# First loads cut smaller, fewer cleared rows and an earlier third block in a talking-heads attention with a dense block behind it

## Chip, cores and metric

One core of one Trainium2 chip runs the whole program in one launch. The metric is the device time in microseconds (us), the median of several runs. Beside it stands one profiled execution, from which all rows below come.

## What is computed

```python
scores = scale * q @ k^T                                  # 4 batches, 12 heads, 448 x 448, depth 64
scores = einsum('bhij,hg->bgij', scores, w_pre)           # heads mixed before the softmax
attn   = softmax(scores, axis=-1)
attn   = einsum('bhij,hg->bgij', attn, w_post)            # heads mixed after it
x      = (attn @ v), heads side by side                   # 1792 x 768
h      = x @ w_in                                         # 768 x 2048
out    = where(h > 0, h, exp(min(h, 0)) - 1) @ w_out      # 2048 x 768
```

The two weights of the dense part come as float64 and are turned into float32 on the chip ("decoding").

## The kernel before

**Blocks and steps.** Each batch is cut into four blocks of rows of the score matrix (`BLK`: 10, 12, 12 and 11 groups of ten rows). A group's ten rows times twelve heads make 120 rows of an on-chip tile, and mixing heads is then one matmul with a 60-row weight per half. The blocks n = 0 to 15 are worked off in 92 steps of two groups each (5, 6, 6, 6 steps for a batch). All of it is written out in one loop, `for j in range(-LOOK, N + 3)`, with `LOOK = 2`, and each engine runs its instructions strictly in that order.

**What a step does.** Step j issues, in this order: the mixed scores of step j+2 (`scores`, L251, with the row maximum on VectorE, L256, and the exponential on ScalarE, L258); the sends of the raw scores made one step before (`send`, L240); the product with the values for a block that is finished (`av`, L303); raw scores of a later block (`qk`, L213 or L220, with copies out of PSUM, L230); the mixing behind the softmax of step j (`post`, L282, whose weight `wz` GpSimd scales, L271) and its copy (`keep_post`, L289); then planned pieces of work.

**Raw scores and how they travel.** `qk(n, hp)` makes block n's raw scores for the head pair hp. For blocks 0 and 1 it uses the float32 queries and keys as they are; from block 2 on queries and keys are first split in a high part (VectorE: `qh`, `kh`, L197, L185) and a low part (GpSimd: `ql`, `kl`, L198, L186). Each head's result is copied to a tile `st` (or, at the start, to a `room` borrowed from tiles that are not yet in use) and sent by a DMA into every twelfth row of one of two tiles `raws`; block n uses `raws[n % 2]`. The first scores of a block need the sends of all twelve heads. Block 0 is sent in two parts, four groups first, then six. Its odd heads go through GpSimd's queue, everything else through SyncE's (SP). Rows of `raws` that no head fills are cleared at the start: before the change whole tiles were, by VectorE and GpSimd, ahead of the sends.

**Where the order comes from.** `RAW_AT` gives the steps of a batch in which a block's raw scores are made (two head pairs at a time), `OUT_AT` those of the product with the values; `plan(j, f)` puts loads and splits into a step. Queries are loaded five steps ahead of their first use and split two steps ahead, the keys' splits stand at the same distance. Values of batch 0 are loaded in steps 2 to 7, one head pair each, through GpSimd's queue.

**Dense part.** `Weights` decodes 48 pieces of the weights in four small steps each (`dec.step()`), in every second step of the attention from 20 on, and then inside `Moe.elu` and the loops behind it; a piece is stored to HBM and loaded again as a weight tile `lo`, which ScalarE and GpSimd split (L509, L510) before TensorE uses it (L593).

Of the kernel before, what the change touches and what calls it, by code (L numbers as in the profile page):

```python
# [126 lines left out]
def attention(ctx, tc, qd, kd, vd, wpre, wpost, xd, dec, moe):  # L127
# [61 lines left out]
    def load_q(n, eng):  # L189
        q2[n] = ld.tile([128, NP, 120], F32, tag="q2", name="q2")  # L190
        eng.dma_start(out=q2[n], in_=qd[blocks[n]])
# [42 lines left out]
    def send(n, out, t0=0, t1=None):  # L234
        t1 = t1 or slots[n]
        raw = raws[n % 2][:, t0:t1, :]
        for h, st in out:
            eng = nc.gpsimd if n == 0 and h % 2 else nc.sync
            lo = FRONT + h
            eng.dma_start(out=raw[lo:lo + (R - 1) * H + 1:H], in_=st[t0 * R:t1 * R])  # L240
# [3 lines left out]
    def scores(n, ts):  # L244
        z = small.tile([128, 2], F32, tag="z", name="z")
        got = []
        ps = [bank("s", mixes) for _ in ts]
        for w in range(2):
            for a in range(len(ts)):
                half = slice(a * 64, (a + 1) * 64)  # L250
                nc.tensor.matmul(  # L251
                    ps[a][w * 64:(w + 1) * 64, :S], wa[half], raws[n % 2][half, ts[0] + w, :],
                    start=True, stop=True)
        for i in range(len(ts)):
            nm = small.tile([128, 1], F32, tag="nm", name="nm", bufs=6)
            nc.vector.tensor_reduce(nm, ps[i][:, :S], op=ALU.max, axis=AX.X, negate=True)  # L256
            p = pp.tile([128, S], F32, tag="p", name="p")
            nc.scalar.activation(  # L258
                p, ps[i][:, :S], AF.Exp, bias=nm, scale=1.0, accum_out=z[:, i:i + 1])
            got.append(p)  # L260
        return got, z
# [61 lines left out]

    warm = pp.tile([128, S], F32, tag="p", name="warm")
    nc.vector.memset(warm, 0.0)
    nc.vector.memset(raws[0][:, :FIRST], 0.0)
    nc.gpsimd.memset(raws[0][:, FIRST:], 0.0)
    nc.gpsimd.memset(raws[1][:, NP:], 0.0)
    k0 = atp.tile([128, NJ * 12 * RH], F32, tag="at", name="k0")[:, :NP * S].rearrange("p (h s) -> p h s", h=NP)
    load_q(0, nc.sync)  # L330
    for hp, eng in ((4, nc.scalar), (2, nc.sync), (0, nc.scalar)):
        eng.dma_start(out=k0[:, hp:hp + 2], in_=kd[0, hp:hp + 2].rearrange("h p s -> p h s"))
        for w in range(2):
            k2[0, hp + w] = k0[:, hp + w]
    load_q(1, nc.sync)
    wa = cst.tile([128, 64], F32, name="wa")
    wb = cst.tile([128, RH // 2], F32, name="wb")
    nc.sync.dma_start(out=wa, in_=wpre)
    nc.sync.dma_start(out=wb, in_=wpost)
    for n in (S, S, 128):  # L340
        nc.tensor.matmul(bank("s", six)[:120, :n], warm[:, :120], warm[:, :n], start=True, stop=True)
    nc.vector.memset(raws[1][:, :NP], 0.0)
    for ps in mixed:
        nc.scalar.copy(ps[64:, 0, NJ - 1], warm[64:, :RH // 2])
        nc.scalar.copy(ps[:64, 1, NJ - 1], warm[:64, :RH // 2])
    nc.vector.tensor_scalar_mul(wa, wa, 1.0 / float(np.sqrt(D)))
    rooms = [vp.tile([128, NJ * CJ], F32, tag="v", name="room")[:120, :S] for _ in range(8)]
    rooms += [xp.tile([128, NP * 120], F32, tag="x", name="room")[:120, :S] for _ in range(2)]
    rooms += [ld.tile([128, S], F32, tag="k2", name="room", bufs=4)[:120] for _ in range(2)]
# [1 line left out]
    for hp in (4, 5, 2, 3, 0, 1):  # L351
        got = keep_qk(0, [(hp, qk(0, hp))], rooms)
        send(0, got, 0, FIRST)
        out += got
    send(0, out, FIRST)
    for hp in range(4):
        send(1, keep_qk(1, [(hp, qk(1, hp))]))
# [15 lines left out]
    OUT_AT = [(6, 8, 10), (12, 14, 16), (18, 20, 22), (23, 25, 27)]  # L373
    for n in range(1, NBL):
        b, i = blocks[n]
        at = [b * ROUND + j for j in (RAW_AT[i] if n > 2 else (None, (0, 0, 0), (2, 4, 6))[n])]
        for u in range(2 if n == 1 else 0, 3):
            qks.setdefault(at[u], []).append((n, u))
        if n > 1:
            plan(max(at[0] - 5, 1 - LOOK), lambda n=n: load_q(n, nc.gpsimd))  # L380
        if n > 1:
            plan(at[0] - 2, lambda n=n: split_q(n, nc.vector.tensor_copy, nc.gpsimd))
        if i == (0 if b else 2):
            for hp in range(NP):
                t = at[hp // 2] - bool(b)
                if b:
                    plan(t - 5, lambda b=b, hp=hp: load_k(b, hp, nc.gpsimd))
                plan(t - 2 + hp % 2, lambda b=b, hp=hp: split_k(
                    b, hp, nc.vector.tensor_copy, nc.gpsimd))
# [6 lines left out]
                for w in range(2):  # L396
                    plan(j + w, lambda b=b + 1, hp=2 * u + w: load_v(b, hp))
    for hp in range(NP):
        plan(hp + 2, lambda hp=hp: load_v(0, hp))

    DENSE = {N - 3: (0, 0), N - 1: (0, 1), N: (1, 0), N + 1: (1, 1), N + 2: (2, 0)}
    sc, nz, ready = {}, {}, []
    for j in range(-LOOK, N + 3):
        if j == N - 10:
            op_ctx.close()
            moe.begin()
            spare = [(moe.ps[0], f"ps{i}") for i in (2, 3)]
        if j >= N - 10:
            mixes = [(ps_s, "s0"), (ps_s, "s1")] if (N - j) % 2 else [(moe.ps[0], "ps0"), (moe.ps[0], "ps1")]
        if j == N - 2:  # L410
            s_ctx.close()
            raw_ctx.close()
            moe.begin_elu()
        if j == N:
            spare = [(ps_t, f"t{i}") for i in range(2)]
        if j in DENSE and j >= N:
            moe.first(*DENSE[j])
        if j + LOOK - 1 in sc:
            nz[j + LOOK - 1] = norm(*sc.pop(j + LOOK - 1))
        if 0 <= j + LOOK < N:  # L420
            sc[j + LOOK] = scores(*steps[j + LOOK])
        for n, out in ready:
            send(n, out)
        for n, u in avs.get(j, ()):
            for w in range(2):
                av(n, 2 * u + w)
            keep_av(n, u)
        ready = [(n, keep_qk(n, [(hp, qk(n, hp)) for hp in (2 * u, 2 * u + 1)], rooms)) for n, u in qks.get(j, ())]
        if j in nz:
            post(nz.pop(j))  # L430
            keep_post(*steps[j])
        if LATE <= j < 3 * ROUND and j % 2 == 0:
            dec.step()
        for f in work.get(j, ()):
            f()
        if N - 10 <= j < N:
            moe.loads(j - (N - 10))
        if N - 7 <= j < N:
            moe.ahead(j - (N - 7))
        if j in DENSE and j < N:  # L440
            moe.first(*DENSE[j])
        if j >= N - 1:
            moe.elu_first(j - N + 1)


class Moe:
# [150 lines left out]
    def elu(self, h, f, u):  # L597
        nc = self.nc

        g = self.ep.tile([128, S], F32, tag="g", name="g", bufs=4)  # L600
        nc.scalar.activation(g, h, AF.Relu, scale=-1.0)  # L601
        e = self.eps.tile([128, 512], F32, tag="e", name="e")[:, :S]
        nc.scalar.activation(e, g, AF.Exp, scale=-1.0)
        nc.scalar.activation(g, g, AF.Tanh, scale=-0.5)
        self.dec.step(3 + (u and f < 4))
        nc.vector.scalar_tensor_tensor(g, e, 1.0, g, op0=ALU.add, op1=ALU.mult)  # L606
        nc.vector.tensor_max(g, g, h)
        self.keep()
        self.last = g, f, u
# [510 lines left out]
```

## Time and profile before

| | us |
|---|---|
| median of 3 runs | 815.98 (814.39 to 818.77) |
| profiled execution, its own time | 811.92 |
| its span, first to last instruction | 810.1 |
| TensorE matmul busy | 780.5 (96%) |
| VectorE, ScalarE, GpSimd busy | 581.2, 509.3, 401.3 |

The 1.8 us between the span and the execution's own time lie around the program. Busy time of TensorE counts matmuls in flight, at whichever of its two clock levels (1.2 and 2.4 GHz) they ran; what ends its idle time is in the waits.

### The profile page before, as it was taken

Reading aid. Unit: us, or ns where it says so; the run is one execution under the profiler, and the core shown is the slowest. Engines: PE = TensorE matmul, PEld = TensorE weight load, DVE = VectorE, ACT = ScalarE, POOL = GpSimd, SP = SyncE. Lnnn points to the kernel's source line nnn. Section 1 sums busy time; section 2 is a strip of 40 time slices with the busy share of each in tenths; the row PEclk is TensorE's granted clock in tenths of the full one; section 3 lists DMA queues with packets and bytes.
Section 4 is the critical chain, followed back from the end, with each engine's and each line's share of the span. In section 5 each row is a group of like instructions: output and inputs, shape, how many; then the busy total and the mean of one; then the engine's idle time right before and its main releaser. Section 6 shows DMA issues by size and latency. Waiting matters only on the chain.

```text
span 810.1 us, 25135 instructions
## 1 busy us (share of the span) xinstructions
PE 780.5 (96%) x10014; PEld 630.4 (78%) x10014; DVE 581.2 (72%) x1082; ACT 509.3 (63%) x1092; POOL 401.3 (50%) x527
## 2 busy tenths in 40 slices
PE   7888998999899989999999999999999999999998
PEld 3355676666676766688799999999999999999997
DVE  5787666877687756667998886766556777688962
ACT  3676877777788768874787772233157576665440
POOL 6575544663557342254777772265238787600000
PEclk9899999999999999999999999999999999999999
DMA  6576577866776665837998879988535768553331
GB/s 196 187 221 216 166 230 241 246 197 202 251 238 184 217 207 157 237 112 244 331 313 273 282 243 340 309 304 300 192 120 190 228 215 268 187 166 116 116 123 58
DMA packets 92749, 174.60 MB, mean 216 GB/s; under 512 B 21792, under 2 KB 59460, under 8 KB 92632
## 3 DMA queue, kind: packets, MB, share of 16 engines
q1 hardware_dynamic: 75288, 113.46, 43.6%
q0 software_dynamic: 16800, 58.61, 22.7%
q8 instruction: 79, 1.29, 0.7%
q10 hardware_dynamic: 544, 0.92, 0.3%
q14 instruction: 38, 0.31, 0.1%
HBM read 94.04 MB, written 39.35 MB: 165 GB/s over the span
## 4 chain that ended last, share of the span: by engine, by line
PE 50%; DVE 1%; DMA 1%; issue 1%; ACT 1%; POOL 0%; DVEq 0%; ACTq 0%
PE y L688 15%; PE y L1042 13%; PE h L980 13%; PE h L593 10%; DMA s<-c 1%; DVE c L94 0%; POOL lo L510 0%; DVE g L606 0%; DVE room L80 0%; POOL gl L616 0%; ACT gh L615 0%; ACT g L601 0%; ACT hi L509 0%; DVE room L85 0%; ACT sq L89 0%
## 5 line engine op out<-in xcount | busy, mean ns | idle before, releaser
L256 DVE TENSOR_REDUCE nm<-s 128x1 f32<-128x448 f32 x180 | 103.8, 618 | 60.8 <-PE s L251 60.5
L258 ACT ACTIVATE p<-s,nm 128x448 f32<-128x448 f32 x180 | 112.6, 631 | 50.3 <-DVE nm L256 49.5
L271 POOL TENSOR_SCALAR wz<-wb,rz 128x60 f32<-128x60 f32 x180 | 79.5, 453 | 106.3 <-DVE rz L267 81.4
L289 ACT COPY at<-mixed 128x480 f32<-128x480 f32 (+1 forms) x184 | 93.3, 566 | 34.3 <-PE mixed L282 32.6
L282 PEld LDWEIGHTS mixed<-wz,p 64*64 64x64 f32 x5040 | 85.1, 135 | 35.0 <-issue 24.6
L282 PE MATMUL mixed<-wz,p 64*64 64x60 f32 x5040 | 98.6, 222 | 7.5 <-issue 6.1
L251 PE MATMUL s<-raw,wa 64*64 64x448 f32 x720 | 93.8, 559 | 12.3 <-DMA raw<-st 5.6
L303 PEld LDWEIGHTS xo<-at,v 128*64 128x64 f32 x1536 | 75.9, 135 | 33.9 <-ACT st L230 24.0
L1042 PE MATMUL y<-part,hi 128*128 128x448 f32 x336 | 96.4, 367 | 0.0
L303 PE MATMUL xo<-at,v 128*64 128x120 f32 (+2 forms) x1536 | 86.8, 263 | 1.6 <-DMA v<-in 1.6
L509 ACT CAST hi<-lo 128x1024 fp32r<-128x1024 f32 (+1 forms) x49 | 47.9, 978 | 41.1 <-PE y L1042 34.2
L593 PE MATMUL h<-xh,lo 128*128 128x448 f32 x192 | 70.7, 368 | 1.9 <-POOL lo L510 1.9
L980 PE MATMUL h<-op,hi 128*128 128x448 f32 x264 | 72.3, 367 | 0.0
L593 PE MATMUL h<-xh,hi 128*128 128x448 f32 x192 | 71.0, 370 | 0.0
L688 PE MATMUL y<-gh,lo 128*128 128x448 f32 x192 | 70.6, 367 | 0.0
L688 PE MATMUL y<-gl,hi 128*128 128x448 f32 x192 | 70.5, 367 | 0.0
L688 PE MATMUL y<-gh,hi 128*128 128x448 f32 x192 | 70.5, 367 | 0.0
L593 PE MATMUL h<-xl,hi 128*128 128x448 f32 x192 | 70.5, 367 | 0.0
L1042 PEld LDWEIGHTS y<-part,hi 128*128 128x128 f32 x336 | 63.0, 188 | 6.3
L510 DVE TENSOR_TENSOR lo<-lo,hi 128x1024 fp32r<-128x1024 f32 x30 | 37.6, 1253 | 42.1 <-ACT hi L509 39.9
L980 PE MATMUL h<-op,lo 128*128 128x448 f32 x240 | 67.3, 367 | 0.0
L1042 PE MATMUL y<-part,lo 128*128 128x448 f32 x168 | 61.8, 368 | 0.0
(121 smaller groups left out, 1647.2 us busy)
## 6 DMA issues: line engine op xcount, KB each, us to landing
raw<-st SPq DMA_DIRECT2D x140, 210.0 KB
w<-in POOLq DMA_DIRECT2D x48, 512.0 KB, 5.9
lo<-s SPq DMA_DIRECT2D x58, 256.0 KB
s<-c POOLq DMA_DIRECT2D x48, 256.0 KB, 5.1
raw<-st SPq DMA_DIRECT2D x36, 175.0 KB
v<-in POOLq DMA_DIRECT2D x24, 256.0 KB, 7.0
lo<-half SPq DMA_DIRECT2D x16, 384.0 KB
lo<-sum SPq DMA_DIRECT2D x12, 512.0 KB
```

Source lines behind the costliest of these rows:

```text
L251: nc.tensor.matmul(ps[a][w * 64:(w + 1) * 64, :S], wa[half], raws[n % 2][half, ts[0] + w, :], start=True, stop=True)
L256: nc.vector.tensor_reduce(nm, ps[i][:, :S], op=ALU.max, axis=AX.X, negate=True)
L258: nc.scalar.activation(p, ps[i][:, :S], AF.Exp, bias=nm, scale=1.0, accum_out=z[:, i:i + 1])
L271: nc.gpsimd.tensor_scalar_mul(wz, wb, rz[:, i:i + 1])
L282: nc.tensor.matmul(mixed[w][half, i, c, :], p[part, j * 64:(j + 1) * 64], wz[part], start=True, stop=True)
L289: nc.scalar.copy(ats[n][:, :, ts[0]:ts[0] + len(ts), w, :], mixed[w][:, :len(ts)].rearrange("p t c n -> p c t n"))
L303: nc.tensor.matmul(ps[hh * 64:(hh + 1) * 64, w * m:(w + 1) * m].rearrange("p (t r) -> p t r", r=HR), vs[blocks[n][0], hp][:, c, hh * 64:(h ...
L509: self.nc.scalar.copy(hi_, f32(lo_))
L593: self.nc.tensor.matmul(h, w[:, ks], x[:, k, :], start=n == 0, stop=n == 3 * NC - 1)
L688: nc.tensor.matmul(y[u], w[:, ks], g[f][:, u, :], start=f == 0 and n == 0, stop=f == NF - 1 and n == 2)
L980: nc.tensor.matmul(y, p[:, ks], x[:, z], start=q < 2 and k == 0 and n == 0, stop=k == KH - 1 and n == 2, skip_group_check=True)
L1042: nc.tensor.matmul(y, w[:, ks], g[:, x], start=begun is None and k == 0 and n == 0, stop=k == FH - 1 and n == 2, skip_group_check=True)
```

## The change

Eight things change.

- **First loads.** The queries of block 0 come in two loads (head pairs 4 and 5, then 0 to 3) instead of one; the keys of pairs 4 and 5 in one load each, one on ScalarE's queue and one on SP's, instead of one load of both; pairs 2 and 3 now go through ScalarE's queue and 0 and 1 through SP's.
- **Cleared rows.** Only the first `FRONT` = 4 rows of each `raws` tile are cleared, over all 5376 columns, both by GpSimd: `raws[0]` ahead of everything, `raws[1]` at the first step. The last four rows are not cleared, and the second half's matmul reads 60 rows instead of 64.
- **Warm-up.** Two matmuls on zeros instead of three (448 and 128 columns).
- **Scaling of `wa`** (the weight that mixes heads) stands on VectorE behind the copies of block 0's raw scores instead of ahead of them.
- **Third block** (n = 2): raw scores in steps 1, 3 and 5 instead of 2, 4 and 6; with them the splits of its queries and of the keys, one step earlier, and the load of its queries, one step earlier. The fourth block's queries are loaded in step 3 instead of 2.
- **Values of batch 0**: loaded in steps 1, 2, 4, 5, 5, 6 instead of 2 to 7.
- **Decoding in the attention** goes on for eight more steps (four more calls).
- **Decoding in `elu`**: the extra call stands at f = 0, 4, 8, 12 instead of f = 0, 1, 2, 3.

```diff
-                half = slice(a * 64, (a + 1) * 64)
+                half = slice(a * 64, a * 64 + (64, RH // 2)[a])
...
-    nc.vector.memset(raws[0][:, :FIRST], 0.0)
-    nc.gpsimd.memset(raws[0][:, FIRST:], 0.0)
-    nc.gpsimd.memset(raws[1][:, NP:], 0.0)
+    nc.gpsimd.memset(raws[0][:FRONT], 0.0)
...
-    load_q(0, nc.sync)
-    for hp, eng in ((4, nc.scalar), (2, nc.sync), (0, nc.scalar)):
-        eng.dma_start(out=k0[:, hp:hp + 2], in_=kd[0, hp:hp + 2].rearrange("h p s -> p h s"))
-        for w in range(2):
-            k2[0, hp + w] = k0[:, hp + w]
+    q2[0] = ld.tile([128, NP, 120], F32, tag="q2", name="q2")
+    nc.sync.dma_start(out=q2[0][:, 4:], in_=qd[0, 0][:, 4:])
+    for hp, n, eng in ((4, 1, nc.scalar), (5, 1, nc.sync), (2, 2, nc.scalar), (0, 2, nc.sync)):
+        if hp == 2:
+            nc.sync.dma_start(out=q2[0][:, :4], in_=qd[0, 0][:, :4])
+        eng.dma_start(out=k0[:, hp:hp + n], in_=kd[0, hp:hp + n].rearrange("h p s -> p h s"))
+    for hp in range(NP):
+        k2[0, hp] = k0[:, hp]
...
-    for n in (S, S, 128):
+    for n in (S, 128):
...
-    nc.vector.memset(raws[1][:, :NP], 0.0)
...
-    nc.vector.tensor_scalar_mul(wa, wa, 1.0 / float(np.sqrt(D)))
...
         out += got
+    nc.vector.tensor_scalar_mul(wa, wa, 1.0 / float(np.sqrt(D)))
     send(0, out, FIRST)
...
-        at = [b * ROUND + j for j in (RAW_AT[i] if n > 2 else (None, (0, 0, 0), (2, 4, 6))[n])]
+        at = [b * ROUND + j for j in (RAW_AT[i] if n > 1 else (0, 0, 0))]
...
-            plan(max(at[0] - 5, 1 - LOOK), lambda n=n: load_q(n, nc.gpsimd))
+            plan(3 if n == 3 else at[0] - 5, lambda n=n: load_q(n, nc.gpsimd))
...
-        plan(hp + 2, lambda hp=hp: load_v(0, hp))
-
+        plan((1, 2, 4, 5, 5, 6)[hp], lambda hp=hp: load_v(0, hp))
+
+    plan(-LOOK, lambda: nc.gpsimd.memset(raws[1][:FRONT], 0.0))
...
-        if LATE <= j < 3 * ROUND and j % 2 == 0:
+        if LATE <= j < 3 * ROUND + 8 and j % 2 == 0:
...
-        self.dec.step(3 + (u and f < 4))
+        self.dec.step(3 + (u and f % 4 == 0))
```

On VectorE, the start of the program stood as follows before (`room` is the copy of a raw score of block 0, `st` of block 1).

```order
L325 MEMSET warm 128x448
L326 MEMSET raw_196 128x1792
L342 MEMSET raw_197 128x2688
L346 TENSOR_SCALAR wa<-wa 128x64
L230 COPY room<-qk 100x448 x6
L230 COPY st<-qk 120x448 x4
```

With the change the same engine begins so:

```order
L325 MEMSET warm 128x448
L230 COPY room<-qk 100x448 x6
L354 TENSOR_SCALAR wa<-wa 128x64
L230 COPY st<-qk 120x448 x4
L256 TENSOR_REDUCE nm<-s 128x1 x2
```

The two clears are gone, and the scaling of `wa`, which waits for a load, stands behind the six copies instead of ahead of them.

On GpSimd (POOL), from the clears to the weights `wz` of the first three steps, before:

```order
L327 MEMSET raw_196 128x3584
L328 MEMSET raw_197 128x2688
L240 DMA raw_196<-room 10x4x448 x6
L240 DMA raw_196<-room 10x6x448 x6
L271 ISA
L271 TENSOR_SCALAR wz<-wb,rz 128x60 x2
L191 DMA q_382<-in 128x720
L271 TENSOR_SCALAR wz<-wb,rz 128x60 x2
L198 TENSOR_TENSOR ql<-q_382,qh 128x720
L186 TENSOR_TENSOR kl<-k_205,kh 128x448
L271 TENSOR_SCALAR wz<-wb,rz 128x60 x2
```

The same stretch with the change:

```order
L326 MEMSET raw_196 4x5376
L240 DMA raw_196<-room 10x4x448 x6
L240 DMA raw_196<-room 10x6x448 x6
L191 DMA q_357<-in 128x720
L401 MEMSET raw_197 4x5376
L271 ISA
L271 TENSOR_SCALAR wz<-wb,rz 128x60 x2
L198 TENSOR_TENSOR ql<-q_357,qh 128x720
L186 TENSOR_TENSOR kl<-k_203,kh 128x448
L271 TENSOR_SCALAR wz<-wb,rz 128x60 x2
L186 TENSOR_TENSOR kl<-k_203,kh 128x448
L271 TENSOR_SCALAR wz<-wb,rz 128x60 x2
```

The load of the third block's queries and the clear of `raws[1]` (`raw_197`) now stand ahead of the first `wz`, and the first splits ahead of the second.

On TensorE the piece of the difference around step 1, between the mixed scores of step 3 (`s`) and the mixing behind the softmax of step 1 (`mixed`), is this:

```order
 L282 MATMUL mixed_199<-wz,p 64x60
 L251 MATMUL s<-raw_196,wa 64x448 x4
+L220 MATMUL qk<-kh,qh 120x448 x2
+L220 MATMUL qk<-kl,qh 120x448 x2
+L220 MATMUL qk<-kh,ql 120x448 x2
+L220 MATMUL qk<-kh,qh 120x448 x2
+L220 MATMUL qk<-kl,qh 120x448 x2
+L220 MATMUL qk<-kh,ql 120x448 x2
 L282 MATMUL mixed_198<-wz,p 64x60
```

These twelve matmuls are the third block's first two head pairs; they stood behind the next step's scores, and the two other groups of twelve move by one step in the same way.

## Rows read from the trace of the kernel before

**Rows 1.** The page: span, and busy time and share of TensorE, and its share of the last chain.

```profile
span 810.1 us, 25135 instructions
PE 780.5 (96%) x10014; PEld 630.4 (78%) x10014; DVE 581.2 (72%) x1082; ACT 509.3 (63%) x1092; POOL 401.3 (50%) x527
```

**Rows 2.** Stretches: us, busy time per engine (instructions), granted clock, DMA share, GB/s.

```profile
5.07:15.09 10.02, 9.96 (x41) 4.84 (x40) 6.47 (x11) 5.32 (x10) 5.97 (x10) 1.00 0.64 181
...
18.74:28.30 9.56, 8.02 (x32) 2.32 (x33) 4.66 (x11) 4.44 (x13) 2.27 (x5) 0.51 0.58 178
28.30:60.39 32.09, 27.74 (x682) 17.06 (x680) 26.26 (x53) 22.31 (x57) 22.70 (x34) 1.00 0.66 209
...
63.48:122.49 59.01, 58.95 (x1452) 40.94 (x1452) 42.05 (x104) 45.10 (x116) 31.37 (x51) 1.00 0.65 203
```

**Rows 3.** TensorE's waits from 0 to 64 us: total us, times, longest.

```profile
PE s L251 <- DMA raw<-st: 3.1, 1, 3.1
PE xo L303 <- DMA v<-in: 1.6, 1, 1.6
...
PE qk L220 <- POOL kl L186: 1.1, 3, 0.5
```

**Rows 4.** Timeline to 19 us: start us, us, engine, line, instruction, [idle before].

```profile
0.72 3.08 POOL L327 MEMSET raw<- 128x3584 f32 x1 [0.29 <-POOLq L1109]
...
5.07 10.02 PE L213 MATMUL qk<-k,q 64*100 64x448 f32 x40
...
8.81 0.20 DVE L346 TENSOR_SCALAR wa<-wa 128x64 f32<-128x64 f32 x1 [2.81 <-DMA wa<-in]
...
8.92 3.83 DVE L230 COPY room<-qk 100x448 f32<-100x448 f32 x6
...
13.04 3.82 POOL L240 DMA_DIRECT2D raw<-room  x7 [0.21 <-issue]
...
18.74 3.27 PE L251 MATMUL s<-raw,wa 64*64 64x448 f32 x16 [3.65 <-DMA raw<-room]
```

**Rows 5.** Line L213: duration of one matmul, min/median/max in ns.

```profile
L213 PE MATMUL qk<-k,q x48: 536/536/1097, 5.1 to 27.6; 64*100 64x448 f32 x24, 64*120 64x448 f32 x24
```

**Rows 6.** DMA from 0 to 30 us: GB/s in 40 slices of 0.75 us; block 0's sends.

```profile
GB/s 0 0 96 363 389 406 389 359 403 384 114 0 96 91 120 132 146 160 139 170 122 211 235 246 196 196 117 141 153 151 122 146 213 210 249 186 211 228 208 237
...
raw<-room POOLq DMA_DIRECT2D x6, 70.0 KB, 3.8
```

**Rows 7.** Timeline from 23 to 38 us: first weights, mixing, splits, second block's scores.

```profile
23.06 0.85 POOL L271 TENSOR_SCALAR wz<-wb,rz 128x60 f32<-128x60 f32 x2 [6.20 <-DVE rz L267]
...
28.30 1.04 PE L282 MATMUL mixed<-wz,p 64*64 64x60 f32 x56
...
30.17 1.78 POOL L198 TENSOR_TENSOR ql<-q,qh 128x720 fp32r<-128x720 f32 x1 [3.98 <-DVE qh L197]
...
31.91 1.13 POOL L186 TENSOR_TENSOR kl<-k,kh 128x448 fp32r<-128x448 f32 x1
...
37.66 0.98 PE L251 MATMUL s<-raw,wa 64*64 64x448 f32 x8 [0.99 <-ACT st L230]
```

**Rows 8.** DMA from 29.5 to 36 us, when SP's sends alone move: the totals.

```profile
DMA packets 949, 1.58 MB, mean 244 GB/s; under 512 B 73, under 2 KB 948, under 8 KB 948
```

**Rows 9.** Timeline from 47 to 64 us: ScalarE, TensorE, SP's sends, TensorE again.

```profile
48.83 1.02 ACT L289 COPY at<-mixed 128x480 f32<-128x480 f32 x2 [1.55 <-POOL kl L186]
...
51.05 0.46 PE L220 MATMUL qk<-kh,qh 64*120 64x448 f32 x2
...
52.64 10.00 SPq L240 DMA_DIRECT2D raw<-st  x8
...
63.48 0.98 PE L251 MATMUL s<-raw,wa 64*64 64x448 f32 x8 [3.10 <-DMA raw<-st]
```

**Rows 10.** TensorE's waits from 372 to 400 us.

```profile
PE h L593 <- POOL lo L510: 1.9, 2, 1.1
```

**Rows 11.** A stretch in the fourth batch, columns as in rows 2.

```profile
297.70:301.00 3.30, 3.30 (x59) 2.52 (x59) 2.71 (x6) 2.29 (x7) 0.00 (x0) 0.50 0.37 130
```

## Prediction

> **What bounds the kernel now.** The page comes first: TensorE is busy for 780.5 of 810.1 us, VectorE for 581.2 and ScalarE for 509.3 [rows 1]. A change pays only where it takes away time in which TensorE stands still or runs slowly, and there are 29.6 us of the first kind in all. The table of stretches says where the start differs from the rest: from 63.48 to 122.49 us TensorE is busy for 58.95 of 59.01 us, but from 28.30 to 60.39 only for 27.74 of 32.09, and from 18.74 to 28.30 at a granted clock of 0.51 [rows 2], the lower of its two levels. The waits up to 64 us name the ends of the idle time: 3.1 us for sent raw scores, 1.6 us for values, 1.1 us for the low parts of keys [rows 3]; the timeline adds 3.65 us ahead of the first mixed scores at 18.74 [rows 4]. Nearly all edits lie in these 64 us. Behind them TensorE is the bound, so what is gained there should be kept to the end, unless a later wait takes it.
>
> The sum is made against the profiled execution, 811.92 us (810.1 of span and 1.8 around it). The median of the three runs is 815.98, that is 4.06 more; I take the gain from the profile and the level from the median.
>
> **First loads, clears and the scaling of wa.** Before, the first matmul of raw scores starts at 5.07 [rows 4] and needs 360 KB of queries and 448 KB of keys. The DMA moved 363 to 406 GB/s from 2.25 us on and some 70 KB earlier [rows 6]: 830 thousand bytes are there by about 4.2 us, and TensorE follows about 0.8 us later. Now 120 KB and 224 KB suffice, with up to as much again of the next key load beside them: 350 to 580 thousand bytes, 3.0 to 3.6 us, so a start at 3.8 to 4.4, say 3.9: 1.2 us sooner. The total of loads is the same, and they are still over by about 8 us.
>
> VectorE waits 2.81 us for wa until 8.81, and only then copies block 0's odd heads, from 8.92 to 12.75 [rows 4]. GpSimd sends them: the sixth of its sends starts near 13.04, and the first mixed scores wait for it until 18.74 [rows 4]. With wa behind the copies and the clears off VectorE, each copy follows its matmul, and since keys come 1.2 us sooner too, the last copy should end near 10.9 instead of 12.75, and the sixth send start near 11.2. If it lands as late as before, 5 us, the first scores start 1.8 us sooner; if it lands like the median of these sends, 3.8 us [rows 6], 3.0 us sooner. The lower end is the keys' 1.2 us. I take **2.4 us**, between the two, because the sends are spread over more time and queue up less.
>
> No row shows a clear of 4 rows. By columns, from 3.08 us for 3584 [rows 4], 5376 columns take 4.6 us; by elements they would take 0.15 us. I take 4.6, the same engine's nearest row read for columns. The first clear then runs to 5.3 us, before GpSimd has anything to send. The second stands ahead of the first `wz`: GpSimd's sends end near 15, the load of queries follows, the clear runs from 15.7 to 20.3, and `wz`, 23.06 before [rows 7], is wanted near 20.7. Even if the sends end at 16.9 as before (13.04 plus 3.82 [rows 4]), `wz` comes at 22.2, and the first mixing that uses it started 5.2 us after `wz` did [rows 7]. So it costs nothing, with that mixing's own wait as cover; without it up to 1.5 us. Behind it `ql` (1.78) and `kl` (1.13 [rows 7]) now stand ahead of the second `wz`: near 24, before step 1 asks for it. The 60-row half changes no duration that I can see a reason for, and 0 is taken.
>
> **Third block earlier.** The twelve matmuls of each pair of head pairs only change places: nothing is added, and the copies and sends go with them. The second block's first scores start at 37.66 [rows 7], behind a stream of sends that runs at 244 GB/s [rows 8], 0.88 us per 210 KB. That stream cannot be hurried, so what the start gains, 2.4 us, is all that I carry to this point (35.2), though by TensorE alone it could be nearer 33.
>
> From 37.66 to 60.39 (22.7 us) the same work follows in both kernels. In it TensorE waits 1.6 us for values [rows 3], whose first two loads now come one step sooner, and ScalarE waits 1.55 us for a low part of keys [rows 9], whose split now comes one step sooner. Both overlap; they are worth 0.5 us (if another load takes the place) to 2.1. I take **1.7**.
>
> Then the 3.1 us for the third block's sends. Its last raw scores were made at 51.05 and its sends began at 52.64 [rows 9]; until 63.48 that is 12.4 us from matmul to use. Now they stand a step earlier, so that a mixing (1.04 [rows 7]), a step's scores and the product with the values, some 3.7 us together, come between: 9.3 us of TensorE work plus 3.7 is 13.0 us against the 12.4 that the transfer took. The wait goes to between 0 and, if the values' loads delay the sends by all of this, 3.1. I take 0.3 left, **2.8** gained. Queries of the fourth block are loaded one step later and are used four steps behind that; 0.
>
> **Decoding.** Four more steps lie in a stretch where TensorE is the bound and VectorE has room; three of the four extra calls in the first rounds of the dense part leave it, where TensorE waits 1.9 us for a split [rows 10]. The bounds are 0 and 1.9; I take **1.0**.
>
> **Sum.** 2.4 + 1.7 + 2.8 + 1.0 = 7.9; for new waits, of which nothing in the trace can speak, 0 to 3, I take 0.9 off. **7.0 us**: 804.9 on the profiled execution's scale, **809.0** on the median's. The bounds together give a loss of 1.3 (1.2 + 0.5 + 0 + 0 - 3) to a gain of 10.2.
>
> **A rule weighed.** The rows show four loads of the start side by side at close to 400 GB/s [rows 6], and one large load is not needed for that rate. The Trainium skill ("DMA: Bandwidth & Descriptors", section "Rules for kernel authors") says the contrary of this edit: many small transfers should be coalesced into a large one; its section on the anatomy of a DMA gives about 2.0 us fixed for each. By that rule, as an estimate, the second key load would not come before 5.9 us, the 1.2 us would be lost, and the sum would be 5.8. The loads here do not wait for each other, so I go by the rows; the rule's case is part of the second rival.
>
> **Rivals.**
> - *The sends bind.* The same bytes have to move in a shorter time, values' loads now fall into the second and third block's sends, and raw scores are again waited for, in step 3 or 9. For it: the DMA share of 0.66 from 28 to 60 us [rows 2], with 244 GB/s as the top of the sends alone [rows 8]. Against it: 12.4 us of transfer against 13.0 of cover. The third block's 2.8 go, and 1 more in step 3: 7.0 - 3.8 = 3.2 gained, 812.8.
> - *The start gains nothing*, since the sends queue behind each other and behind the loads as before, or since each smaller load takes as long as the large one did (the first edit does not do what it says). 7.0 - 2.4 = 4.6 gained, 811.4.
> - *The clock stays up* at 17.8 us, because the idle time ahead of the first scores shrinks from 3.65 to about 2.4 us. 8.02 us busy at 0.51 [rows 2] hold about 4 us that could go, but data set the pace: 2 us on top, 9.0 gained, 807.0.
> - *Slower: the clock falls once more.* Place: steps 1 to 4, where new idle time of about 2 us ahead of the second block's scores is possible. After 3.65 us of idle the clock was 0.51 for the next 9.6 us [rows 2, 4], while in the fourth batch it was 0.50 for 3.3 us [rows 11]; at this level a matmul of raw scores takes 1097 ns instead of 536 [rows 5]. A fall of 10 us costs up to 5, 814.0; from 14 us on (7.0 over one half) the kernel is slower than before. The Trainium skill ("TensorE: Matmul & The Clock Gate", "What's actually happening") has the lower clock as the default, which activity releases; the trace agrees, with 0.51 behind the idle time and 1.00 behind the busy stretch. Against it: 3.1 us of idle at 60.39 were followed by 1.00 [rows 2, 9]. The shorter warm-up belongs here too: matmuls of raw scores take its place at once.
>
> **How the numbers follow.** Forecast (806.5 to 811.2) 0.45; the sends bind 0.22; the start gains nothing 0.15; the clock stays up 0.10; the clock falls 0.08. The range from 804.0 to 814.5 takes in all but the ends, some 0.15: a gain of 10.2 with the clock's 2 gives 803.8, and beyond 814.5 lie a clock that is low for more than 11 us and the worst of the sends. About 0.5%, 4.1 us, can be told from no change here. Faster by more: the forecast, the clock that stays up, 0.09 of the start's case and 0.04 of the sends', 0.68. Slower by more: 0.05 of the clock and 0.02 of the sends, 0.07. Within: 0.25.
>
> **What the changed profile would show.** VectorE's first copy directly behind its matmul, with no wait for wa; first mixed scores at 16 to 17; second block's at about 35; no wait above 0.5 us for values; third block's first scores at 56 to 57 without a wait above 1 us; and the same distance from there to the first product of the dense part as before, to 1 us. The forecast is wrong if a clear of 4.6 us turns up as TensorE's wait for `wz`, if a raw-score wait of 2 us or more stands in step 3 or 9, or if the 7 us are there at 64 us and gone at 370.

## The result and the profile after

The changed kernel takes 802.68 us in the median of six executions (799.08 to 811.09), the kernel before 815.18 us in six beside them, 12.5 us more. The ratio on record is not that of these medians (0.9847): it leaves out executions in a slower state that any kernel falls into at times, and is 0.9888, with a 95% interval from 0.9845 to 0.9932, or 9.1 us less (5.5 to 12.6). Repeated beside 31 executions of the kernel before, it gave 0.9926 (0.989 to 0.9962), 6.0 us less. The forecast was 7.0. The profiled execution is one of the long ones, 808.0 us, and shows a stall that the kernel's second profile does not have, so both are read below.

The page after, first lines (answering [rows 1]):

```profile
span 806.2 us, 25127 instructions
...
PE 770.4 (96%) x10012; PEld 628.2 (78%) x10012; DVE 573.2 (71%) x1080; ACT 509.9 (63%) x1092; POOL 403.7 (50%) x527
```

TensorE is busy for 10.1 us less than before, yet the span is only 3.9 us shorter: idle time has grown from 29.6 to 35.8 us. Less busy time for the same matmuls (two records fewer, by the shorter warm-up) means that they ran faster. For the most part that is not the change's doing: in the second profile of the kernel before TensorE is busy for 773.7 us, 6.8 less than in its first (see the last section). TensorE's waits up to 64 us (answering [rows 3]; total, times, longest):

```profile
PE s L251 <- DMA raw<-room: 15.1, 3, 8.2
...
PE qk L213 <- DMA k<-in: 0.4, 1, 0.4
```

The waits for values, for the third block's sends and for low parts of keys are gone. For block 0's and block 1's sends stand 15.1 us, in three waits; the first of them, 3.79 us, stood there before with 3.65. TensorE's timeline shows where (start us, us; answering [rows 4, 7, 9]):

```profile
4.08 9.07 PE L213 MATMUL qk<-k,q 64*100 64x448 f32 x40 [0.42 <-DMA k<-in]
16.93 3.26 PE L251 MATMUL s<-raw,wa 64*64 64x448 f32 x16 [3.79 <-DMA raw<-room]
23.31 1.33 PE L251 MATMUL s<-raw,wa 64*64 64x448 f32 x8 [3.11 <-DMA raw<-room]
...
42.50 1.77 PE L251 MATMUL s<-raw,wa 64*64 64x448 f32 x8 [8.17 <-DMA raw<-room]
...
62.94 1.04 PE L282 MATMUL mixed<-wz,p 64*64 64x60 f32 x56
63.98 0.98 PE L251 MATMUL s<-raw,wa 64*64 64x448 f32 x8
```

The first raw scores start 1.0 us sooner and the first mixed scores 1.8 us sooner. But step 2's scores, at 23.31, come hardly sooner than before (23.55), and the second block's wait 8.17 us, until 42.50. The third block's scores then follow without any wait, at 63.98 against 63.48. The stretches of the long wait and behind it (columns as in [rows 2], the granted clock third from the end):

```profile
34.34:42.50 8.16, 0.00 (x0) 0.00 (x0) 1.39 (x2) 1.19 (x4) 2.88 (x6) 0.69 0.60 166
42.50:63.98 21.48, 21.40 (x484) 13.85 (x485) 14.18 (x35) 15.50 (x40) 12.65 (x21) 0.88 0.59 178
```

The granted clock falls during the 8 us of idle time, and part of the next 21 us runs at the lower level, 1.2 GHz. What TensorE waited for is seen in the DMA's rate from 30 to 46 us, 0.4 us a slice:

```profile
GB/s 211 242 197 206 202 224 215 211 229 184 179 125 267 262 239 214 201 241 206 256 238 269 247 142 137 101 49 49 47 43 43 19 25 27 22 27 27 22 27 9
```

From 40.4 us on only 43 to 49 GB/s move, then 19 to 27: a fifth and a tenth of the 244 GB/s of a full stream [rows 8]. The semaphores of the sends issued from 22.7 to 35.5 us show the same: each send has ten landings, and nine came 1.7 to 6.5 us ahead of the last. The last one of all that the scores at 42.50 waited for came at 42.46, and its ninth at 36.37. By this, one of the DMA engines that carry the sends was behind and had the rest alone. In the kernel's second profile the same sends have their last landing only 0.1 to 1.5 us behind the ninth.

VectorE's copies of block 0's odd heads follow their matmuls, and are done at 10.84 us instead of 12.75:

```profile
5.97 0.62 DVE L230 COPY room<-qk 100x448 f32<-100x448 f32 x1 [4.64 <-PE qk L213]
7.21 3.63 DVE L230 COPY room<-qk 100x448 f32<-100x448 f32 x5 [0.61 <-PE qk L213]
```

GpSimd's clears and the first weights:

```profile
0.73 4.57 POOL L326 MEMSET raw<- 4x5376 f32 x1 [0.29 <-POOLq L1110]
16.32 4.57 POOL L401 MEMSET raw<- 4x5376 f32 x1
21.23 0.85 POOL L271 TENSOR_SCALAR wz<-wb,rz 128x60 f32<-128x60 f32 x2 [0.35 <-DVE rz L267]
```

A clear of 4 rows goes by its columns, 4.57 us, and nobody waits for it. And TensorE's waits from 368 to 400 us (answering [rows 10]), 0.3 us instead of 1.9:

```profile
PE h L594 <- POOL lo L511: 0.3, 1, 0.3
```

### The profile page after: what moved, and what is told of

It is laid out like the page before. It is cut to its first block, busy times and chain, and to the rows that moved or that the text cites. A ratio compares the mean times of both kernels' runs of the same rounds, so it can differ in the third digit from the quotient of the medians.

```text
span 806.2 us, 25127 instructions
## 1 busy us (share of the span) xinstructions
PE 770.4 (96%) x10012; PEld 628.2 (78%) x10012; DVE 573.2 (71%) x1080; ACT 509.9 (63%) x1092; POOL 403.7 (50%) x527
## 4 chain that ended last, share of the span: by engine, by line
PE 89%; DMA 4%; issue 2%; ACT 1%; DVE 1%; SPq 1%; POOL 0%; ACTq 0%; DVEq 0%; POOLq 0%
PE y L689 14%; PE h L594 13%; PE y L1043 13%; PE h L981 13%; PE mixed L282 10%; PE xo L303 9%; PE s L251 8%; PE qk L220 7%; DMA raw<-room 2%; DMA raw<-st 2%; PE qk L213 1%; SPq L240 1%; ACT at L289 1%; DMA k<-in 0%; ACT p L258 0%
## 5 line engine op out<-in xcount | busy, mean ns | idle before, releaser
L251 PE MATMUL s<-raw,wa 64*64 64x448 f32 (+1 forms) x720 | 92.8, 560 | 18.0 <-DMA raw<-room 15.1
```

The source lines that it names most:

```text
L251: nc.tensor.matmul(ps[a][w * 64:(w + 1) * 64, :S], wa[half], raws[n % 2][half, ts[0] + w, :], start=True, stop=True)
```

## The experiments

The table gives for each kernel the ratio to the kernel before with its 95% interval, and three starts on TensorE in its profile (us): the second block's first scores, the third block's, and the first product of the dense part. "Start" means loads, clears, scaling of `wa`, the 60-row half and the warm-up together. Each start is read from one profile; the two profiles of the kernel before differ by 0.5 us at the third block and by 3.4 us at the dense part.

| kernel | ratio | second block | third block | dense |
|---|---|---|---|---|
| before, first profile | 1 | 37.66 | 63.48 | 349.7 |
| before again (b1_before) | 0.9989 (0.9947-1.0031) | 38.59 | 64.02 | 346.3 |
| decoding alone (a4_decode) | 1.0034 (0.9993-1.0074) | 37.99 | 63.80 | 356.9 |
| start alone (a2_start) | 0.9988 (0.9945-1.003) | 37.97 | 64.13 | 349.1 |
| values alone (b3_values) | 0.9974 (0.9933-1.0016) | 37.15 | 61.87 | 346.0 |
| raw scores alone (b2_raw) | 0.9941 (0.9904-0.9978) | 36.77 | 60.48 | 345.9 |
| raw scores and values (a3_third) | 0.9913 (0.9873-0.9953) | 36.68 | 58.02 | 348.0 |
| those and start (b4_no_decode) | 0.9894 (0.9838-0.9951) | 35.24 | 56.02 | 350.2 |
| changed, first profile | 0.9888 (0.9845-0.9932) | 42.50 | 63.98 | 352.6 |
| changed again (a1_again) | 0.9926 (0.989-0.9962) | 35.98 | 56.29 | 350.6 |
| changed, ScalarE sends (c1_act) | 0.9911 (0.9876-0.9947) | 35.20 | 55.56 | 350.6 |

**The changed kernel again.** No edit.

> The changed kernel once more, for a second profiled execution. In the first one TensorE waited 8.17 us for the second block's sends (34.34 to 42.50), the third block's first scores came at 63.98, 0.5 us later than before, and the first dense product at 352.6, 2.9 us later; the 3.9 us gained in the whole arose behind it, although the timed executions are some 9 us faster than before. Theory A (that execution was out of the ordinary: one of the DMA engines that carry the sends lagged): second block's first scores at 35 to 38, third block's at 56 to 60, first dense product at 342 to 348. Theory B (the order of the sends makes the wait every time, and the gain is made in the dense part): 41 to 44, 62 to 65 and 350 to 354 again. Time by both: 802.7, from 799 to 806.

```profile
35.98 0.98 PE L251 MATMUL s<-raw,wa 64*64 64x448 f32 x8 [1.20 <-DMA raw<-st]
...
56.29 0.98 PE L251 MATMUL s<-raw,wa 64*64 64x448 f32 x8
...
226.86 1.77 PE L251 MATMUL s<-raw,wa 64*64 64x448 f32 x8 [8.41 <-DMA raw<-st]
```

At the third block theory A holds, 7.2 us sooner than in the first profile of before. At the dense part it fails: 350.6. Most of the difference is one wait of 8.41 us for sends, now at the second block of the third batch. Of three of the sends that it was for, issued from 207.6 to 211.2 us, the last landing came 4.1, 5.7 and 6.9 us behind the ninth. The DMA row, 214 to 228 us in slices of 0.35 us, ends in the same tail:

```profile
GB/s 209 266 244 180 312 305 217 196 153 263 188 187 351 266 94 255 215 235 201 256 172 258 274 206 246 266 205 154 154 133 236 210 236 128 189 92 46 26 36 15
```

So the long wait is not bound to the change's place. The kernel with only the decoding changed, whose sends are those of before, has one of 7.1 us, until 234.40.

**The start alone.** The kernel before with the diff's edits up to the scaling of `wa`, and the second clear.

> Only the start is changed (queries and keys in smaller loads, 4-row clears, wa scaled behind the copies, shorter warm-up); third block, values' loads and decoding as before. Theory A: first mixed scores at 16.9, second block's at 35 to 37, the third block's wait stays at 3 us or grows by what is gained; 1 to 3 us faster than before (0.996 to 0.999). Theory B: second block's scores at 41 to 44 behind a wait of 6 us or more, and the time the same or up to 4 us slower (1.000 to 1.005).

```profile
17.53 3.27 PE L251 MATMUL s<-raw,wa 64*64 64x448 f32 x16 [4.74 <-DMA raw<-room]
...
37.97 1.77 PE L251 MATMUL s<-raw,wa 64*64 64x448 f32 x8 [3.10 <-DMA raw<-st]
...
64.13 0.98 PE L251 MATMUL s<-raw,wa 64*64 64x448 f32 x8 [1.54 <-DMA raw<-st]
```

The first mixed scores come some 1.2 us sooner, the second block's do not, the third block's do not, and the time is the same, so neither theory's second block came (35 to 37 or 41 to 44). By itself the start gains nothing that can be measured.

**Raw scores and values.**

```diff
-        at = [b * ROUND + j for j in (RAW_AT[i] if n > 2 else (None, (0, 0, 0), (2, 4, 6))[n])]
+        at = [b * ROUND + j for j in (RAW_AT[i] if n > 1 else (0, 0, 0))]
...
-            plan(max(at[0] - 5, 1 - LOOK), lambda n=n: load_q(n, nc.gpsimd))
+            plan(3 if n == 3 else at[0] - 5, lambda n=n: load_q(n, nc.gpsimd))
...
-        plan(hp + 2, lambda hp=hp: load_v(0, hp))
+        plan((1, 2, 4, 5, 5, 6)[hp], lambda hp=hp: load_v(0, hp))
```

> Only the third block's raw scores at steps 1, 3, 5, the fourth block's queries at step 3 and the earlier loads of values; start and decoding as before. Theory A: second block's scores at 37 to 38 as before, the waits of 1.6 us for values and of 3.1 us for the third block's sends gone, its first scores at 58 to 60; 3.5 to 5.5 us faster (0.993 to 0.996). Theory B: a wait of 2 us or more for raw scores in step 3 or behind the second block's first scores takes the place; 0 to 1.5 us faster (0.998 to 1.000).

```profile
56.94 1.04 PE L282 MATMUL mixed<-wz,p 64*64 64x60 f32 x56
58.02 0.98 PE L251 MATMUL s<-raw,wa 64*64 64x448 f32 x8
```

No wait stands ahead of the third block's scores. These three lines alone give 5.5 us at this point (63.48 to 58.02) and 7.1 us in the time (0.9913 of 811.19, interval 3.8 to 10.3), as much as the whole change gives; theory A had 3.5 to 5.5.

**The two halves of it.** First with the old `load_v` line, then with that line alone.

> Only the third block's raw scores at steps 1, 3, 5 with its queries and the fourth block's; values loaded as before, start and decoding as before. Theory A (the sooner sends are the gain): the 3.1 us wait for the third block's sends goes, the values are waited for as before (1.6 us) or up to 2 us longer, third block's first scores at 59.5 to 61; 2 to 4.5 us faster (0.9945 to 0.9975). Theory C (the values' loads are half of it: without them the product with the values, which now stands ahead of the third block's scores, holds them up): 62 to 64, 0 to 1.5 us faster (0.998 to 1.000).

```profile
50.56 1.58 PE L303 MATMUL xo<-at,v 128*64 128x100 f32 x16 [1.85 <-DMA v<-in]
...
60.48 0.98 PE L251 MATMUL s<-raw,wa 64*64 64x448 f32 x8
```

> Only the values' loads are sooner. Theory A: the wait of 1.6 us for values goes and stands again, up to 1.6 us longer, ahead of the third block's first scores (63 to 64): 0 to 0.5 us faster (0.9995 to 1.000). Theory C: third block's scores at 61.5 to 62.5 and 1.5 to 3 us faster (0.996 to 0.998).

```profile
51.98 0.73 PE L220 MATMUL qk<-kh,qh 64*120 64x448 f32 x1 [1.86 <-ACT p L258]
...
61.87 0.98 PE L251 MATMUL s<-raw,wa 64*64 64x448 f32 x8
```

The sooner raw scores are worth 3.0 us at the third block and leave the wait for values; the sooner values are worth 1.6 us, and a wait of 1.86 us for ScalarE stands behind them. Together they are worth 5.5, a little more than the 4.6 of the parts. For the raw scores theory A holds; for the values theory C holds in the profile, while the time (0.9974, interval up to 1.0016) can't tell it from nothing.

**Decoding, alone and taken out.**

```diff
-        if LATE <= j < 3 * ROUND and j % 2 == 0:
+        if LATE <= j < 3 * ROUND + 8 and j % 2 == 0:
...
-        self.dec.step(3 + (u and f < 4))
+        self.dec.step(3 + (u and f % 4 == 0))
```

> Only the decoding is changed (its steps go on for eight steps more, and three calls of the dense part's first rounds are left out). Theory A: the two waits for low parts between 372 and 400 us (1.9 us) go, and nothing else changes: 1 to 2 us faster (0.9975 to 0.999). Theory B (the gain is made in the dense part): 5 us or more (under 0.994).

> The changed kernel with the decoding of before: start and third block together. Against the third block alone (0.9913, 805.2) it shows what the start is worth beside it, against the changed kernel (0.9926, 805.0) what the decoding is. Theory A (the start's 1.7 us pass the second block's sends only in part): second block's first scores at 35 to 37, third block's at 56.5 to 59, 7 to 9 us faster (0.989 to 0.9915). Rival (the start gains nothing): third block's first scores at 58 to 60, 5 to 7 us faster (0.9915 to 0.994). Decoding: a wait for low parts of 0.9 to 1.9 us again between 372 and 400; if it is worth that, the ratio is 0.001 to 0.002 above the changed kernel's.

The three calls are moved to later rounds, not left out. With the new decoding alone the wait for low parts between 368 and 400 us is 0.3 us; in the changed kernel without it that wait is back:

```profile
PE h L594 <- POOL lo L511: 1.8, 2, 0.9
```

The times show no gain: 1.0034 alone, and 0.9894 without against 0.9888 and 0.9926 with. In the second of these kernels the start's part shows: with the start the third block's scores come at 56.02 instead of 58.02. The times, 0.9894 against 0.9913, can't tell that from nothing.

**The kernel before again.** No edit. It settles whose the slower matmuls of its first profile are (last section).

> The kernel before once more, for a second profiled execution. Its first one needed 118.7 us from first to last product of the dense part's second stage, where the five others profiled since needed 115.5 to 115.7, and 2.9 us more in all than the profile of the changed kernel from the first dense product on. If that slower pace is the execution's own: 115.5 here, second block's first scores at 37 to 38, third block's at 63 to 64 behind a wait of 3 us, span 806 to 810, ratio 1.000. If it belongs to the kernel before: 118 to 119 again.

```profile
53.52 0.46 PE L220 MATMUL qk<-kh,qh 64*120 64x448 f32 x1 [1.89 <-ACT p L258]
...
64.02 0.98 PE L251 MATMUL s<-raw,wa 64*64 64x448 f32 x8 [0.67 <-DVE rz L267]
```

The third block's scores come at 64.02, as expected, but not behind 3 us of waiting for sends, and no wait for values stands ahead of them either. Instead TensorE waits 2.58 us for the second block's sends and 1.89 us for ScalarE. So the two waits that the forecast read off its one profile (3.1 and 1.6 us) are not there each time. What repeats is the time of the third block's scores: 63.48 to 64.13 in all five profiles with the old third block and the old loads of values.

**The first parts of block 0's odd heads from ScalarE's queue.**

```diff
-            eng = nc.gpsimd if n == 0 and h % 2 else nc.sync
+            eng = (nc.scalar if t1 == FIRST else nc.gpsimd) if n == 0 and h % 2 else nc.sync
```

> The changed kernel, with the first parts of block 0's odd heads sent by ScalarE's queue instead of GpSimd's. In the three profiles with the new start the first mixed scores wait for sends until 16.6 to 17.5 us, those of step 2 until 23.3 or 23.4, and the second block's until 35.2 to 42.5. Theory Q (GpSimd's queue slows the sends of both queues): first mixed scores at 14 to 16, step 2's at 20 to 22, second block's at 33 to 35, third block's at 55 to 57.5; 1 to 3 us faster than the changed kernel (0.986 to 0.990 of the kernel before). Theory E (the sends' bytes and their engines bind, from whatever queue): 16.5 to 17.5, 23 to 24 and 35 to 36 again, and the changed kernel's time (0.989 to 0.993).

```profile
18.96 4.76 PE L251 MATMUL s<-raw,wa 64*64 64x448 f32 x24 [4.59 <-DMA raw<-room]
35.20 0.98 PE L251 MATMUL s<-raw,wa 64*64 64x448 f32 x8 [0.56 <-DMA raw<-st]
```

The first mixed scores come 2 us later than in the changed kernel, step 2's follow them without a wait, and the second block's stand at 35.20 all the same. So the time of the first mixed scores does not matter here: the second block's scores wait for their sends (0.56 us) in any case. Of theory E the second block's 35 to 36 and the changed kernel's time hold; its first two times do not, nor does theory Q. The Trainium skill ("DMA: Bandwidth & Descriptors", "Rules for kernel authors") says that spreading DMAs over several issuing engines brings no bandwidth; this run agrees.

**A step earlier in later batches.**

```diff
-    RAW_AT = [(-10, -8, -6), (-4, -2, -1), (1, 3, 5), (7, 9, 11)]
+    RAW_AT = [(-10, -8, -6), (-4, -3, -2), (1, 3, 5), (7, 9, 11)]
```

> The changed kernel, with the raw scores of the second block of the later batches at steps -4, -3, -2 before their batch instead of -4, -2, -1. In all profiles TensorE waits at these blocks' first scores: 0.6 to 2.1 us near 117 to 126, up to 8.4 near 218 to 234, up to 2.1 near 311. Theory A (the sends' distance to their use is too short there): none of the three above 0.5 us; 1.5 to 4 us faster than the changed kernel (0.985 to 0.9895). Rival (the DMA is full there, with a share near 0.9, and the sends start only when the buffer's last reader is done): the same waits to 1 us, and the changed kernel's time (0.989 to 0.993).

The ratio is 0.9872 (0.982 to 0.9923), not to be told from the changed kernel's. The profile has TensorE waiting 8.2 us for sends between 64 and 350 us, 7.1 of them at once; its execution is the longest of that kernel, 813.02 us, and its waits are not read further. Whether the edit helps is open.

**Both kernels without the dense part.** The lines that run it, but for its first five rounds of products, are replaced by one copy and one store.

> The kernel before without the dense part: everything behind the first five up-products of it is left out, so that one execution ends soon after 360 us and the scatter of the dense part is not in its time. By itself: 358 to 368 us. It is to be compared with the changed kernel cut at the same place.

> The changed kernel, cut at the same place as the one before. Profiles of the four uncut kernels with the new start and the sooner third block have the first dense product at 350 to 353 us, those of the kernel before and of single edits at 346 to 357, although the former are 7 to 8 us earlier at the third block. Theory G (the gain is made in the first 64 us and kept; the later waits of those profiles are chance): 5 to 8 us less than the cut kernel before, in the median of the executions. Theory N (what is gained at 64 us is waited for again by 350, and the gain of the whole comes from the dense part): 0 to 2 us less. In between: part of it is given back in the attention part.

The medians of six executions each are 390.21 us (387.96 to 395.39) and 386.90 us (382.09 to 388.91), 3.3 us less. The first lies 22 us above what was expected of it, for what is left of the dense part runs for 37.5 us in both profiles. The start of the dense part in them is 351.4 and 346.7:

```profile
L593 PE MATMUL h<-xh,hi x30: 362/368/475, 351.4 to 376.7; 128*128 128x448 f32 x30
```

```profile
L594 PE MATMUL h<-xh,hi x30: 362/368/481, 346.7 to 372.0; 128*128 128x448 f32 x30
```

By the medians that is the middle case: a part of what is gained at the third block is kept to the end of the attention part. But the executions of each kernel scatter over some 7 us; by an estimate from that scatter the difference is uncertain by 3 us either way, so neither theory G nor theory N is ruled out.

## Why the prediction came out as it did

The time and the sign were right, 0.9914 forecast against 0.9888 and 0.9926; on the forecast's scale (815.98) these are 806.8 and 809.9 us. The sizes of the single edits up to the third block held, but for the start by itself; decoding and what is kept behind the third block did not. That the total fits is in part luck: the third block gave 1.0 us more than was taken, and new waits took at least 1.5 us more.

- **Third block earlier.** 2.8 us for the sends measured 3.0; 1.7 us for values and keys measured 1.6; together 5.5 instead of 4.5. This is the change's gain, and the time confirms it: 0.9913 with these lines alone. The sizes are shown; that just these two named waits had to go is not, since the second profile of the kernel before reaches the same place without them.
- **First loads, clears and the scaling of `wa`.** The keys' 1.2 us measured 1.0, the clear 4.57 us against 4.6, and `wz` at 21.23 against 20.7, waited for by nobody. The first mixed scores, forecast at 16 to 17, came at 16.93 and 16.57 (17.55 and 17.53 in the kernels with the same start). By the estimate from the rule of the Trainium skill on coalescing ("DMA: Bandwidth & Descriptors", "Rules for kernel authors") the second key load would not have come before 5.9 us. It did: TensorE uses it from 4.95 us on, and makes raw scores for 9.07 us from 4.08 on without a wait. The section on the anatomy of a DMA has its 2.0 us for DMAs that GpSimd issues; these loads are issued by SP and ScalarE. What failed is the sentence that carries this gain on by itself. Alone it is worth nothing at the third block, as the rival *the start gains nothing* had it; beside the sooner raw scores it is worth 2.0 us in the profiles (58.02 to 56.02), near the 2.4 taken. The ScalarE run shows that the first scores' time is not what is carried on. What is, stays open: in the start's own profile the stream of sends begins as soon as in the changed kernel's (6.37 us against 6.48 and 6.41), and the second block's scores still come at 37.97.
- **The second block's first scores** were forecast at 35.2; they came at 35.20 to 35.98 in three profiles, at 36.27 in that of the step earlier, at 38.30 in that of the cut kernel, and at 42.50 in the one that the result gave. There the rival *the sends bind* came true in full, with 8.17 us, through one late DMA engine and with a fallen clock behind it. That was chance: the wait is not in the second profile, and a wait like it stands elsewhere in other kernels, the one with the old sends among them. The forecast's own sign, a raw-score wait of 2 us or more in step 3, was met in this profile.
- **The clock.** From 16 to 28 us it is 0.57 and 0.72 in the two profiles of the kernel before, 0.72 and 0.57 in those of the changed kernel: it belongs to the execution, and the rival *the clock stays up* has nothing for it. *The clock falls once more* came only behind the wait of 8.17 us; 0.88 over the next 21.48 us is some 5 us at the lower level, 2.6 us lost by an estimate from it.
- **New waits, 0.9 us.** This term was too small. Among the kernels with the old third block (before twice, decoding, start, cut before) the first dense product comes 282 to 293 us behind the third block's first scores, 286.9 in the mean. Among those with start and third block both new (changed twice, without decoding, ScalarE, cut after) it is 288 to 295, 292.0 in the mean. So 5.1 us are given back in these profiles, where the forecast had the same distance to 1 us. The waits between 66 and 346 us account for it, by two kinds that were there already: for sends, and "issue", which is nothing that the profile shows. Their sum is 7.6 to 13.8 us in the first group (mean 9.5) and 12.7 to 17.1 in the second (mean 14.3). At the third block the second group is 5.7 us ahead in the mean (58.1 against 63.8), so in these profiles little is left at the dense part; in the times of the cut kernels 3.3 us are left, that is 2.4 given back; and the one pair of cut profiles gives nothing back (4.9 us ahead at the third block, 4.7 at the dense part). So the term is 2.4 (uncertain by 3) to 5.1 where 0.9 was taken. Being ahead at the third block can't be all of it: the changed kernel's first profile is not ahead there and has 13.5 us of these waits. Whether the new order must meet more of them, or met them by chance, stays open. The prediction's other sign of being wrong, 7 us there at 64 and gone at 370, was met in the changed kernel's second profile.
- **Decoding, 1.0 us.** The wait went, as said, but the time shows nothing of it: alone 1.0034, with an interval that reaches down to 0.9993, so less than 0.6 us. From the first dense product to the end the profiles of kernels with the new decoding take 453.6 or 454.1 us, those with the old one 455.0 to 456.1, executions with slower matmuls apart. What takes this away ahead of the dense part was not found.

What the parts measured, 3.3 us kept to the dense part and at most 0.6 of decoding, makes some 4 us. The whole was measured at 6.0 and 9.1 us, with intervals that begin at 3.1 and 5.5: the first agrees, and against the second 1.5 us or more have no explanation here but the 3 us by which the 3.3 is uncertain. One slip is in the prediction's sum: the upper bounds add to 10.1, not 10.2.

## What to carry to other kernels

A step that is moved ahead of a wait pays by the amount of work that comes to stand between transfer and use; it can be read off the timeline before, and here its forecast was right to 0.2 us. Take two profiles before a wait is counted by its name: another execution came to the same time by other waits. A first consumer that starts sooner need not pay: here it started 1.2 us sooner for nothing, and 2 us later without loss. Ask when the last transfer lands that the next stage waits for. And a gain in one stretch should not be carried to the end at full size where later stretches have waits of their own: cut the kernel behind the stretch and time both.

## What the runs showed of the hardware

**One late DMA engine.** While only sends of ten rows move, their queue takes 64.5% of 16 engines' time in the kernel before from 29.5 to 36 us:

```profile
q1 hardware_dynamic: 948, 1.57, 64.5%
```

That is about ten of 16 (10.3), fully busy. The Trainium skill ("DMA: Bandwidth & Descriptors", "Why a DMA increments its semaphore by 16 and not by 1") says that a DMA takes the largest number of engines, up to 16, that divides the slowest dimension of both its sides, which is ten for ten rows; the share agrees. A send has landed when its last landing has, 42.46 us for the wait that ended at 42.50, and so one engine that is behind holds up everything, 8.17 and 8.41 us in the two profiles of the changed kernel. A send whose slowest dimension had 16 parts was not tried.

**One queue issues a send every 0.85 us.** In the changed kernel SP's sends of 70 KB (6.5 to 11.1 us) and of 210 KB (20.1 to 26.6 us) take the same time to issue (ns, min/median/max; the seventh of the first row is one of 105 KB):

```profile
L240 SPq DMA_DIRECT2D raw<-room x7: 748/748/2436, 6.5 to 11.9; - x7
```

```profile
L240 SPq DMA_DIRECT2D raw<-st x8: 755/758/999, 20.1 to 26.6; - x8
```

Where nothing else holds them up they begin 0.85 us apart. At 210 KB that makes 253 GB/s, close to the 244 of the full stream. So the prediction's "cannot be hurried" has a rival: the issuing queue may set the stream's rate as well as the ten engines. Sends of the second block over two queues were not tried.

**Two paces at one granted clock.** From 480 to 590 us, within the dense part, the granted clock is 1.00 in both profiles of the kernel before, yet the first runs 535 products and the second 549 (stretch, us, TensorE busy):

```profile
480.00:590.00 110.00, 110.00 (x535) 99.74 (x534) 74.30 (x99) 33.91 (x52) 44.95 (x66) 1.00 0.82 277
610.00:690.00 80.00, 80.00 (x391) 73.03 (x390) 60.14 (x94) 53.04 (x95) 64.40 (x50) 1.00 0.71 227
```

```profile
480.00:590.00 110.00, 110.00 (x549) 102.75 (x549) 79.26 (x103) 37.22 (x61) 46.45 (x63) 1.00 0.80 269
610.00:690.00 80.00, 80.00 (x391) 72.98 (x390) 59.06 (x93) 51.36 (x92) 62.70 (x48) 1.00 0.75 239
```

That is 205.6 against 200.4 ns each; from 610 us on both run 391. The slower pace is that of the first profile of before, of the raw scores alone and of the step earlier, 3 of 12 uncut profiles, so it belongs to the execution and not to a kernel; what causes it is open. It made the first comparison of two profiles look as if the dense part had gained almost 7 us.

**Waits for instructions.** In three profiles (changed, before again, without decoding) all 20 waits of over 0.6 us between 64 and 370 us that are put down to "issue", most of them at mixings, end 2.3 to 2.9 us after a 16 KB packet of the DMA queue named instruction began; there are 79 such packets in an execution, one in some 10 us. The longest, in the kernel without decoding, and the queue's line from 292.9 to 296.2 us:

```profile
296.12 0.67 PE L282 MATMUL mixed<-wz,p 64*64 64x60 f32 x20 [3.20 <-issue]
```

```profile
q8 instruction: 1, 0.02, 2.6%
```

TensorE seems to wait there for its own instructions; no run here tested it.
